# Tile 16's g transposed on TensorE instead of by DMA in a fused attention, feed-forward and soft mixture-of-experts kernel

## The chip, the cores and the metric

The kernel runs on one core of a Trainium2 chip. The time is the device time of one execution in microseconds, as the median of three runs; all times below without a unit are microseconds. Five engines work side by side, each on its own queue of instructions in program order: TensorE (PE, with its weight loads shown apart as PEld), VectorE (DVE), ScalarE (ACT), GpSimd (POOL) and SyncE (SP), which here only issues transfers.

## The reference

Three stages follow each other. Windowed causal attention over 4 batches, 8 heads, 576 positions and 64 columns a head gives x with 2304 tokens and 512 columns. A feed-forward layer of width 2048 follows, and then a soft mixture of 8 experts with 4 slots each.

```python
# attention: each query sees the 64 positions up to and including its own
attn = softmax(where(mask, q @ k.T / sqrt(D), -1e9))
x = (attn @ v)                                # 2304 x 512
# feed-forward
h = x @ w_in                                  # 2304 x 2048
g = h * tanh(log1p(exp(h)))                   # Mish
x = g @ w_out                                 # 2304 x 512
# soft mixture of experts
logits = x @ phi                              # 2304 x 32
d = softmax over tokens(logits);  slot_input = d.T @ x
slot_out[e] = relu(slot_input[e] @ w1[e]) @ w2[e]
out = softmax over slots(logits) @ slot_out
```

## The kernel before

The 2304 tokens are 18 tiles of 128, t = 0 to 17. The kernel never forms x after the feed-forward layer. It multiplies w_out by phi beforehand (wphi), so that the logits come straight from g, and it accumulates d.T @ g in A (32 slots by 2048 columns of g, kept as 128x512), to be multiplied by w_out only at the end.

For each tile TensorE makes four projections h of 128x512 (L587, twelve matmuls each, in f16 with a high and a low part). ScalarE applies Mish (L593) into u. GpSimd writes the high f16 part of g (L607), VectorE the low part (L612), both into `gg`: for each half of the 2048 columns a tile of 128 x 2 x 1024. In tile 17 this goes in pieces of 512 columns, in the others of 1024. The logits (L690, L692) need g with its columns on the partitions, `gT`, so `gg` has to be transposed. There are two ways. For tiles below `PET`, SP issues one DMA transpose for each half (`t_tr`, L618). For the others TensorE transposes 128x128 blocks into a PSUM bank (`p_tr`, L625, tiles `pghT` and `pglT`), and VectorE or ScalarE copies the bank into `gT` (`p_trev`, L630). Which of the two copies, goes by the piece's number and `VGA`.

```python
if t < P["PET"]:
    done[t, h] = [f"tr{t}_{h}"]
    op(f"tr{t}_{h}", "SP", 3.1, t0 + 12 + 2 * h, lambda t=t, h=h: t_tr(t, h), ...)
    continue
for i in mine:                       # pieces of this half
    for y, w_ in enumerate(("gh", "gl")):
        ev = "ACT" if (y == 0) == (i in P["VGA"]) else "DVE"
        op("p" + nm, "PE", 0.56 * n / 1024, t0 + 20, lambda a_=a_: p_tr(*a_), ...)
        op("v" + nm, ev, ..., lambda a_=a_, ev=ev: p_trev(*a_, ev), ...)
```

Behind the logits a softmax over tokens runs block by block. Tiles 0 to 13 make seven blocks of two, tiles 14 to 17 one block each, so that block 9 is tile 16 and block 10 is tile 17. A block goes: logits `lg` (L690, L692) to `lgt` (L696, L697, and a copy at L702), transposed into `lt` (L711, in block 10 L714), a running maximum `mrun` (L721, L724), exp (L731), the factor between the old and the new maximum (L739), transposed back as `et` (L744), split into two f16 parts (L749, L753), multiplied with g into the bank `A` (L766), and added to the accumulator (L779).

After block 10 the accumulator is transposed (At, L846) and multiplied by w_out (si, L858). Then come the experts, whose weights are 64 loads of 512 KB (`w`, L831) on SP: eh (L892, loads 0 to 31) and eo (L924, loads 32 to 63), and the output tiles fo (L977) with their stores (L989).

The order on every engine is set when the program is built. A planner (`Plan.emit`) plays the work through with estimated costs and priorities, takes the ready operation of the lowest priority number, and writes the instructions in that order. Big buffers are slots of a common pool of 49 (`s`), PSUM has 8 banks (`b`). A load can be issued only into a slot that is free in the plan, and the instruction then waits for the last reader of that slot. The slots of w_out are read last by si. Where the planner finds TensorE without ready work in certain stretches, one of them from the last projection to the first eh matmul, it writes a filler: a matmul of 128x256 into a bank of its own that nobody reads (`fill`, L194, named `pad`). Once written, a filler is an instruction like any other.

Of the kernel before, what the change touches and what calls it, by code (L numbers as in the profile page):

```python
# [24 lines left out]
PRM = dict(  # L25
    FOP=70.175, SUMA=1, XA=3, WHA=8, KEEP=7, MOSTA=0, WQ=478.64, WQ_SP=0.317, A0=-1.816, A1=6.022, AK=11,
    A2=17.918, LEAD=24.658, W0=-29.34, W_SP=5.541, W_DEC=12.468, AT=-40.0, WS=26.932, WS_SP=-0.001, T2=47.76,
    TT=15.744, WOT=72.383, WOT_SP=5.03, WO=3.842, WO_SP=1.043, NU=9, NGC=14, MOST=5, NSC=3, FAST=18, PET=17,
    SINGLE=14, MOSTL=8, LATE=31, RB=10, W2C=((0, 128), (128, 256), (384, 128)), QUART=17, VGA=[1, 3], TP=8.139,
    BL=34.953, NRM=18, VP=(-11.89, -6.08, 4.77, 5.5), CB=-54.142, KL=-1.956, NX=4, TM=(8.06, 15.01, 37.19, 38.77),  # L30
    TM_M=(-2.41, -13.01, 29.97, 14.64),
# [3 lines left out]
class Plan:  # L35
# [20 lines left out]
    def op(self, name, eng, cost, prio, fn, deps=(), get=(), rel=(), table=None, spare=False):  # L56
        assert name not in self.index, name
        self.index[name] = len(self.ops)
        need = list(Counter(p.rstrip("!^") for _, p in get).items())
        self.ops.append((name, eng, cost, prio, fn, list(deps), list(get), list(rel), table, spare, need))  # L60
        for _, p in get:
            if p[-1] in "!^":
                self.left[p] += 1
        for k in rel:
            self.refs[k] += 1
# [94 lines left out]
def body(tc, a):  # L160
# [7 lines left out]
    with ctx:  # L168
# [342 lines left out]

        TT, T2 = P["TT"], P["T2"]
        wot, wp = {}, {}
# [119 lines left out]
        for t in range(NT):  # L633
            t0 = T2 + TT * t
            last = [f"x{t // 2}"]
# [48 lines left out]
        def b_logit(b, j, h):  # L684
            n = len(BLOCKS[b])
            if j == 0 and h == 0:
                lg[b] = bank(f"lg{b}", [128, n, 64])
            t = BLOCKS[b][j]
            for k in range(8):
                PE.matmul(lg[b][:, j], lhsT=gT[t, h][:, 0, k], rhs=wphi[:, 8 * h + k], start=(h == 0 and k == 0), stop=False)  # L690
            for k in range(8):
                PE.matmul(lg[b][:, j, 0:32], lhsT=gT[t, h][:, 1, k], rhs=wphi[:, 8 * h + k, 0:32], start=False, stop=(h == 1 and k == 7))  # L692
# [88 lines left out]
        for b in range(NBLK):  # L781
            n = len(BLOCKS[b])
            e = T2 + TT * BLOCKS[b][-1] + 6 - (P["BL"] if BLOCKS[b][-1] > 15 else 0)
            late = e + 30
            prev = lambda n: [f"{n}{b - 1}"] if b else []
            two = lambda n: [f"{n}{b - 2}"] if b > 1 else []
            for j, t in enumerate(BLOCKS[b]):
                for h in range(2):
                    before = [f"lg{b}_{j}_0"] if h else [f"lg{b}_0_1"] if j else []
                    op(f"lg{b}_{j}_{h}", "PE", 0.43, e - TT * (n - 1 - j) - 2 * (1 - h), lambda b=b, j=j, h=h: b_logit(b, j, h), ["wpl"] + done[t, h] + before,  # L790
                       get=[] if before else [(f"lg{b}", "b")], rel=[f"gT{t}_{h}", f"GT{t}_{h}"])
# [14 lines left out]
            if b:  # L806
# [5 lines left out]

        TE = T2 + TT * NT
        wo, w = {}, {}
        W2C = P["W2C"]
        W2 = w2_parts(W2C)
        decode_ops("wo", a["w_out"], 16, lambda j: (j, 0), wo, lambda j: T2 + TT * (P["WO"] + P["WO_SP"] * j),
                   lambda j: T2 + TT * (P["WO"] + P["WO_SP"] * j) + 4, ["wpl"], "s", "POOL")
# [321 lines left out]
def w2_parts(cols):  # L1140

    return [(c, i, kf, 256 // d) for c, (f, d) in enumerate(cols) for i in range(2) for kf in range(0, 8, 256 // d)]
# [51 lines left out]
```

## Time and profile before

| | us |
|---|---|
| median of 3 runs | 397.94 |
| lowest and highest | 397.88, 398.8 |
| the profiled execution | 398.63 |
| its span, first to last instruction | 396.8 |

The busy times of the engines over that span are 383.6 for TensorE, 268.6 for VectorE, 275.8 for ScalarE and 97.2 for GpSimd. The mean granted clock of TensorE is 0.986 of full speed. A share of busy time is a mean over stages; what counts for a change is the stretch that it touches. Matmuls are pipelined and their ends are modelled, so the distance from one start to the next tells more than the duration of one row. In the chain of waits every step is released by the one before it, or follows it on the same engine.

### The profile page before, as it was taken

The numbers are of one execution on the slowest core, as the hardware profiler recorded it, in microseconds if no ns is written. First come the engines' busy times: TensorE is split into PE (matmuls) and PEld (weight loads), VectorE is DVE, ScalarE is ACT, GpSimd is POOL, SyncE is SP. The second block draws the span as 40 slices with busy tenths as digits, with TensorE's granted clock in tenths as the row PEclk, the third lists the DMA queues.
The fourth block names the chain that finished last, engine by engine and source line by source line (L and its number), as shares of the span: only waits on it lengthen the run. The fifth ranks groups of instructions, "written<-read, shape, count | busy, mean of one in ns | idle before, by whom it ended". The sixth has DMA issues, their size and how long they took to land.

```text
span 396.8 us, 10326 instructions
## 1 busy us (share of the span) xinstructions
PE 383.6 (97%) x4245; PEld 227.2 (57%) x4245; DVE 268.6 (68%) x579; ACT 275.8 (69%) x461; POOL 97.2 (24%) x82
## 2 busy tenths in 40 slices
PE   8999999999999999999999999999999999998982
PEld 6887758555465565566455644444454457636552
DVE  1799888879998969669899977455343374342342
ACT  1677799799986899878898399999655653102131
POOL 0243420205762222247140412121211240100000
PEclk9999999999999999999999999999999999999986
DMA  7999997131599784368999899999998889699997
GB/s 266 403 411 405 393 378 266 59 123 40 101 233 279 276 283 161 116 157 213 219 162 217 173 275 252 292 283 261 265 220 244 244 247 367 249 412 408 405 358 232
DMA packets 100686, 102.67 MB, mean 259 GB/s; under 512 B 74016, under 2 KB 81312, under 8 KB 100640
## 3 DMA queue, kind: packets, MB, share of 16 engines
q1 hardware_dynamic: 100640, 102.02, 85.9%
q8 instruction: 33, 0.54, 0.5%
q14 instruction: 13, 0.11, 0.1%
HBM read 79.46 MB, written 4.72 MB: 212 GB/s over the span
## 4 chain that ended last, share of the span: by engine, by line
PE 89%; DMA 4%; DVE 3%; issue 2%; ACT 0%; SPq 0%; DVEq 0%
PE h L587 47%; PE pad L194 6%; PE px L398 5%; PE pt L385 4%; PE eo L924 4%; PE eh L892 3%; PE s L332 3%; PE A L766 3%; DMA v<-in_vL 3%; PE lg L690 2%; PE lg L692 2%; PE fo L977 1%; DMA q<-in_qL 1%; PE gram_v L374 1%; PE s L323 1%
## 5 line engine op out<-in xcount | busy, mean ns | idle before, releaser
L587 PE MATMUL h<-wh,xx 128*128 128x512 f16 x576 | 184.3, 379 | 0.0
L587 PEld LDWEIGHTS <-xx 128*128 128x128 f16 x864 | 80.4, 98 | 86.4 <-issue 1.8
L587 PE MATMUL h<-wl,xx 128*128 128x512 f16 x288 | 109.1, 379 | 0.0
L364 POOL TENSOR_TENSOR p<-p,st 128x512 f32<-128x512 f32 x36 | 45.7, 1289 | 121.9 <-DVE st L344 34.1
L607 POOL TENSOR_SCALAR gg<-u,sc 128x1024 f16<-128x1024 f32 (+1 forms) x38 | 47.7, 1261 | 108.8 <-ACT u L593 86.1
L593 ACT ACTIVATE u<-h,sc 128x512 f32<-128x512 f32 x72 | 48.4, 686 | 28.0 <-PE h L587 23.4
L612 DVE SCALAR_TENSOR_TENSOR gg<-u,sc,gg 128x1024 f16<-128x1024 f32 (+1 forms) x38 | 50.3, 1332 | 13.8 <-POOL gg L607 13.8
L593 ACT ACT_TABLE_LOAD x41 | 52.6, 1283 | 2.0 <-PE h L587 1.3
L350 ACT ACTIVATE p<-s,st 128x128 f32<-128x128 f32 x144 | 41.8, 377 | 2.8 <-DVE st L344 2.5
L194 PE MATMUL pad<-wphi 128*64 128x256 f16 x259 | 36.5, 290 | 0.9 <-DVE wphi L204 0.9
L194 PEld LDWEIGHTS <-wphi 128*64 128x64 f16 x259 | 27.7, 116 | 5.5 <-issue 2.1
L390 ACT COPY pts<-pt 128x512 f32<-128x512 f32 x36 | 20.9, 588 | 11.4 <-PE pt L385 8.3
L341 DVE TENSOR_REDUCE st<-s 128x4 f32<-128x512 f32 x36 | 24.6, 683 | 5.4 <-PE s L332 5.4
L274 ACT ACT_TABLE_LOAD x19 | 24.4, 1283 | 1.0 <-PEq L1187 0.7
L356 DVE TENSOR_REDUCE st<-p 128x4 f32<-128x512 f32 x34 | 22.9, 674 | 2.4 <-ACT p L350 2.4
L385 PE MATMUL pt<-cst,p 128*128 128x128 f32 x144 | 21.6, 278 | 0.0
L398 PE MATMUL px<-pts,v 128*64 128x64 f32 x576 | 21.4, 225 | 0.0
L398 PEld LDWEIGHTS px<-pts,v 128*64 128x64 f32 x576 | 18.9, 138 | 3.7 <-issue 3.1
L332 PE MATMUL s<-k,q 64*64 64x128 f32 x576 | 18.8, 269 | 0.4 <-DMA q<-in_qL 0.4
L385 PEld LDWEIGHTS pt<-cst,p 128*128 128x128 f32 x144 | 16.1, 141 | 5.3 <-issue 3.0
L332 PEld LDWEIGHTS s<-k,q 64*64 64x64 f32 x576 | 16.9, 133 | 1.9 <-issue 0.7
L924 PE MATMUL eo<-w,hT 128*32 128x128 f32 (+1 forms) x384 | 16.9, 317 | 1.0 <-issue 1.0
(175 smaller groups left out, 491.8 us busy)
## 6 DMA issues: line engine op xcount, KB each, us to landing
w<-in_wL SPq DMA_DIRECT2D x64, 512.0 KB, 6.6
v<-in_vL SPq DMA_DIRECT2D x18, 512.0 KB, 8.3
wir<-in_w_in SPq DMA_DIRECT2D x16, 512.0 KB, 9.7
wtr<-in_w_outT SPq DMA_DIRECT2D x16, 512.0 KB, 4.9
wor<-in_w_out SPq DMA_DIRECT2D x16, 512.0 KB, 5.2
k<-in_kL SPq DMA_DIRECT2D x12, 512.0 KB, 8.8
q<-in_qL SPq DMA_DIRECT2D x9, 512.0 KB, 10.2
out<-ob SPq DMA_DIRECT2D x17, 256.0 KB, 3.9
```

What stands on the lines that cost most here:

```text
L194: PE.matmul(pad, lhsT=hot, rhs=hot.unsqueeze(1).to_broadcast([128, 4, 64]), start=True, stop=True)
L332: PE.matmul(st_[t][h][64 * c:64 * c + 64, p], lhsT=qt[t // 2][r, t % 2, p, 64 * c:64 * c + 64], rhs=kt[g // 3][r, p, 64 * (g % 3):64 * (g ...
L341: DVE.tensor_reduce(stat[t][:, 0, 4 * h:4 * h + 4], st_[t][h], AX.X, ALU.max)
L350: ACT.activation(pr[t][:, h, p], st_[t][h][:, p], AF.Exp, scale=0.125, bias=stat[t][:, 0, 4 * h + p:4 * h + p + 1], accum_out=(stat[t][:, ...
L364: (POOL if t < P["NRM"] else DVE).tensor_tensor(pr[t][:, h], pr[t][:, h], r, ALU.mult)
L385: PE.transpose(q[:, p], pr[t][:, h, p], ident)
L398: PE.matmul(x[64 * h:64 * h + 64, p, f], lhsT=vt[t][:, c, 64 * (2 * p + h):64 * (2 * p + h) + 64], rhs=ptS[t][:, h, p, f], start=True, sto ...
L587: PE.matmul(ph[t, m], lhsT=xh[t][:, l, kk], rhs=r[m][:, kk], start=(kk == 0 and i == 0), stop=(kk == 3 and i == 2))
L593: ACT.activation(ub[t, h][:, m % 2], ph[t, m], AF.Mish, scale=col(INVH + 4 * PART[t] + m))
L607: POOL.tensor_scalar(o, u, col(CP + PART[t]), 1.0, ALU.mult, ALU.mult)
L612: DVE.scalar_tensor_tensor(gg[t, h][:, 1, c:c + n], flat(ub[t, h], c, n), col(CP + PART[t]), gg[t, h][:, 0, c:c + n], ALU.mult, ALU.subtract,)
L924: PE.matmul(tl["o", c][32 * j:32 * j + 32], lhsT=tl[f"hT{i}"][:, 128 * (kf + k) + 32 * j:128 * (kf + k) + 32 * j + 32], rhs=v[:, j, k], st ...
```

## The change

One number changes: `PET` from 17 to 16. Tile 16's two halves are then transposed on TensorE as tile 17's are. Tile 16 has pieces of 1024 columns, so that there are four groups of 8 transposes and four evictions of 128x1024, two on VectorE and two on ScalarE. All priorities are the same as before.

```diff
-    WOT_SP=5.03, ..., MOST=5, NSC=3, FAST=18, PET=17,
+    WOT_SP=5.03, ..., MOST=5, NSC=3, FAST=18, PET=16,
```

The planner then writes another order from tile 17's second projection on. Up to there the order is the same on every engine, and from At on it is the same again.

On SP, among the weight loads, before and after (`gT_0`, `gT_1` are the two halves of tile 16):

```order
L831 DMA w_4372<-in_wL 128x1024
L618 DMA_TRANSPOSE gT_0_4392<-gg_0_4360 128x16x128
L831 DMA w_4421<-in_wL 128x1024
L831 DMA w_4458<-in_wL 128x1024
L831 DMA w_4470<-in_wL 128x1024
L618 DMA_TRANSPOSE gT_1_4483<-gg_1_4426 128x16x128
L831 DMA w_4511<-in_wL 128x1024
```

```order
L831 DMA w_4372<-in_wL 128x1024
L831 DMA w_4419<-in_wL 128x1024
L831 DMA w_4445<-in_wL 128x1024
L831 DMA w_4460<-in_wL 128x1024
L831 DMA w_4485<-in_wL 128x1024
```

The two transposes are gone, and the loads follow each other.

On ScalarE, from tile 17's first Mish on, before and after (u_0, u_1 belong to tile 17; gT_1_4496 and gT_0_4483 belong to tile 16, e_4599 and e_4565 to block 9):

```order
L593 ACTIVATE u_0_4460<-h_0_4398,sc 128x512
L593 ACTIVATE u_0_4460<-h_1_4414,sc 128x512
L593 ACTIVATE u_1_4501<-h_2_4472,sc 128x512
L593 ACTIVATE u_1_4501<-h_3_4493,sc 128x512
L630 COPY gT_0_4529<-pghT_1_4522 128x512
L630 COPY gT_0_4529<-pglT_0_4531 128x512
L630 COPY gT_1_4567<-pglT_2_4571 128x512
L630 COPY gT_1_4567<-pghT_3_4606 128x512
L731 ACT_TABLE_LOAD
L731 ACTIVATE e_4599,bst_4618<-lt_4603,mrun_76 128x128
```

```order
L593 ACTIVATE u_0_4447<-h_0_4396,sc 128x512
L593 ACTIVATE u_0_4447<-h_1_4412,sc 128x512
L630 COPY gT_1_4496<-pghT_1_4472 128x1024
L630 COPY gT_0_4483<-pglT_0_4462 128x1024
L593 ACTIVATE u_1_4536<-h_2_4500,sc 128x512
L731 ACT_TABLE_LOAD
L731 ACTIVATE e_4565,bst_4576<-lt_4568,mrun_76 128x128
L593 ACT_TABLE_LOAD
L593 ACTIVATE u_1_4536<-h_3_4554,sc 128x512
L739 ACT_TABLE_LOAD
L739 ACTIVATE bst_4576<-mrun_75,mrun_76 128x1
L630 COPY gT_0_4594<-pghT_1_4589 128x512
```

The new evictions stand ahead of the third Mish, and block 9's exp stands between the third and the fourth.

On TensorE, around block 9's lt, before and after:

```order
L194 LDWEIGHTS wphi
L194 MATMUL pad_4579<-wphi 64x256
L711 MATMUL lt_4603<-cst,e_4599 128x128
L625 LDWEIGHTS gg_1_4503
L625 MATMUL pghT_3_4606<-idh,gg_1_4503 128x128
```

```order
L587 LDWEIGHTS xx_3576
L587 MATMUL h_3_4554<-wh_1441,xx_3576 128x512
L711 MATMUL lt_4568<-cst,e_4565 128x128
L587 LDWEIGHTS xx_3576
L587 MATMUL h_3_4554<-wh_1441,xx_3576 128x512
```

It stood among fillers behind the projections, and stands between the two halves of the last projection. The 32 new transposes stand between tile 17's second and third projection. Between the last projection and At there are 61 rows of L194 before and 81 after, and between At and si there are 7 in both.

## Rows read from the trace of the kernel before

**Rows 1.** The page: TensorE's busy time, and the chain's shares by engine.

```profile
PE 383.6 (97%) x4245; PEld 227.2 (57%) x4245; DVE 268.6 (68%) x579; ACT 275.8 (69%) x461; POOL 97.2 (24%) x82
...
PE 89%; DMA 4%; DVE 3%; issue 2%; ACT 0%; SPq 0%; DVEq 0%
```

**Rows 2.** Busy time by stage; columns as in the first line.

```profile
core 0: us, PE busy (x) PEld busy (x) DVE busy (x) ACT busy (x) POOL busy (x), PEclk, DMA share, GB/s
314.00:324.60 10.60, 10.60 (x72) 4.71 (x71) 5.50 (x8) 6.80 (x8) 4.22 (x6) 1.00 0.85 236
324.60:338.30 13.70, 13.70 (x177) 10.32 (x175) 6.90 (x25) 5.38 (x12) 1.57 (x2) 1.00 0.96 354
```

**Rows 3.** The chain, 317 to 340: start, length, what.

```profile
318.30 6.48 PE h L587 x30
324.78 0.45 PE pghT L625 x8
...
327.65 0.26 PE lt L711
...
328.13 0.77 PE pad L194 x6
...
333.50 0.76 PE A L766 x12
334.26 0.17 PE et L744
334.43 1.97 PE pad L194 x17
...
337.17 1.21 PE pad L194 x10
338.38 0.59 PE At L846 x4
```

**Rows 4.** Timeline of ScalarE, 317 to 335: start, length, instruction, idle before.

```profile
318.81 1.52 ACT L593 ACTIVATE u<-h,sc 128x512 f32<-128x512 f32 x2
322.23 0.69 ACT L593 ACTIVATE u<-h,sc 128x512 f32<-128x512 f32 x1 [1.90 <-PE h L587]
...
328.77 1.28 ACT L731 ACT_TABLE_LOAD   x1
330.07 0.37 ACT L731 ACTIVATE e<-lt,mrun 128x128 f32<-128x128 f32 x1
330.33 0.19 ACT L731 ACTIVATION_READ_ACCUMULATOR e<-lt,mrun 128x1 f32 x1
```

**Rows 5.** Timeline at 359 to 361: evictions of 128x1024 f16 on VectorE and ScalarE.

```profile
359.95 0.69 DVE L1044 COPY cT<-ct 128x1024 f16<-128x1024 f16 x1
...
360.84 1.01 ACT L1044 COPY cT<-ct 128x1024 f16<-128x1024 f16 x1
```

**Rows 6.** Timeline: g of tile 17's last piece on GpSimd and VectorE.

```profile
325.60 0.69 POOL L607 TENSOR_SCALAR gg<-u,sc 128x512 f16<-128x512 f32 x1
...
327.05 0.75 DVE L612 SCALAR_TENSOR_TENSOR gg<-u,sc,gg 128x512 f16<-128x512 f32 x1
```

**Rows 7.** Timeline of SP's queue: tile 16's transposes, and loads behind si.

```profile
311.06 2.02 SPq L618 DMA_TRANSPOSE gT<-gg  x1
...
319.93 1.75 SPq L618 DMA_TRANSPOSE gT<-gg  x1
...
342.17 1.75 SPq L831 DMA_DIRECT2D w<-in_wL  x4
```

**Rows 8.** Waits of SP's queue, 330 to 348: total, times, longest.

```profile
SPq L831 <- PE si L858: 5.4, 3, 4.7
```

**Rows 9.** The line L831, 371 to 372: the last weight load.

```profile
L831 SPq DMA_DIRECT2D w<-in_wL x1: 327/327/327, 371.4 to 371.4; - x1
...
DMA to landing us min/median/max: 10.1/10.1/10.1
```

**Rows 10.** The chain, 317 to 397: a gap, and the last eo matmuls.

```profile
364.20 1.00 issue
...
384.50 1.49 PE eo L924 x48
```

More of the change, by code (lines that the diff above doesn't have):

```diff
@@ L27 @@
     A2=17.918, LEAD=24.658, W0=-29.34, W_SP=5.541, W_DEC=12.468, AT=-40.0, WS=26.932, WS_SP=-0.001, T2=47.76,
-    TT=15.744, WOT=72.383, WOT_SP=5.03, WO=3.842, WO_SP=1.043, NU=9, NGC=14, MOST=5, NSC=3, FAST=18, PET=17,
+    TT=15.744, WOT=72.383, WOT_SP=5.03, WO=3.842, WO_SP=1.043, NU=9, NGC=14, MOST=5, NSC=3, FAST=18, PET=16,
     SINGLE=14, MOSTL=8, LATE=31, RB=10, W2C=((0, 128), (128, 256), (384, 128)), QUART=17, VGA=[1, 3], TP=8.139,
```

## The prediction

> **What bounds the kernel now.** I read the page first. TensorE is busy for 97% of the span, and the chain that ended last runs on TensorE for 89% of it, against 4% on DMA [rows 1]. An average hides stages, so next I read busy time in the two stretches that the change touches: the last projections of tile 17 (314.0 to 324.6) and what follows them up to the transposition of the accumulator, At (324.6 to 338.3). In both, TensorE is busy for the whole stretch, at a granted clock of 1.00, which is the 2.4 GHz level [rows 2]. Whatever is added to TensorE's queue there is therefore paid for, unless something else in that queue becomes shorter.
>
> The second stretch needs a closer look, because much of its busy time is not work. The chain in order of time shows 30 projections in 6.48, then groups of L194 between the small steps of the softmax blocks: 6, 17 and 10 of them, for example [rows 3]. These are fillers: matmuls into a bank that nobody reads, written into the program by the planner for as long as it believes that TensorE waits. They stand in a fixed number. If the result they bridge comes early, TensorE still has to run them. So the length of this stretch is the sum of its queue as long as no real wait outlasts the fillers, and the number of fillers counts as work.
>
> Last I read what comes behind At. The weight loads of the tail (L831) wait for the si matmuls, 5.4 in all and 4.7 at the longest [rows 8]; four of them go out from 342.17 on [rows 7]. The last one leaves at 371.4 and lands 10.1 later, at 381.5 [rows 9]. TensorE reaches its last group of eo, which needs that load, at 384.50 [rows 10]: 3.0 after it is there. So the end hangs on when TensorE gets through At and si; the stream of loads is let go by the same si and follows.
>
> **The change, part by part.**
>
> *The transposes added.* Tile 16 has two halves of 2 x 1024 columns of f16, which make 32 transposes of 128x128. TensorE runs 8 of them in 0.45 in tile 17 [rows 3], so 32 take 4 x 0.45 = 1.80. They stand behind the first projections of tile 17, where TensorE has no idle time [rows 2], so all 1.80 is on the path. Those projections are not shortened by anything.
>
> *The logits and the transposed scores of block 9 (tile 16).* One half of the logits and the one lt matmul move from the stretch with fillers to before the end of the projections. They are the same instructions. Between projections a row has no filler group around it; the lt with its surroundings took 0.26 among fillers [rows 3] and cannot take less than nothing. I take no gain, and keep 0.3 of gain in the range (two group boundaries of about 0.1 each, and some of the 0.26).
>
> *The fillers.* Counting L194 from the last projection to At, the order has 61 before and 81 after; the 7 behind At stay. A group of 17 takes 1.97 and one of 10 takes 1.21 [rows 3], so a filler takes (1.97 - 1.21) / 7 = 0.109. Twenty more take 2.17. By the group of 6 in 0.77 [rows 3] a filler would be 0.128, and twenty 2.57, which I keep as the upper end. I take 0.109, since the added ones stand in groups of 4 to 16, and the number of groups hardly changes.
>
> *ScalarE.* It gets two evictions of 128x1024, each 1.01 by the nearest row, the eviction of the same shape at L1044 [rows 5]. They stand between the second and the third Mish of tile 17. In the trace there is a pause there: the pair of Mish that starts at 318.81 is over at 320.33, and the third starts at 322.23 [rows 4], when its projections are done. These now end 1.80 later for the transposes and 0.45 earlier for the half of block 9's logits that no longer stands ahead of them, so that Mish starts at about 323.6. The 2.02 of eviction, from about 320.5 on, ends at 322.6: hidden. Then the order puts block 9's exp between the third and the fourth Mish, which costs two more table loads of 1.28 [rows 4]: one to Exp, one back, with a third one to Exp after the fourth Mish in the place of the one that stood behind the evictions before.
>
> *Whether that makes TensorE wait.* The projections end at 324.78 + 1.80 + 0.45 (half the logits) + 0.11 (lt) - about 0.1 = 327.0. Block 9's lt is out at 325.7; its maximum takes VectorE about 0.8, its exp 0.37 and the accumulator read 0.2 [rows 4], so ScalarE is free at about 327.0. Table load 1.28 and Mish 0.69 [rows 4]: 329.0. GpSimd 0.69 and VectorE 0.75 [rows 6]: 330.6. TensorE needs this result for the last transposes of tile 17. In its queue it has by then, from 327.0 on: 24 transposes (1.35), 28 fillers in four groups (about 3.5), the et (0.17), block 9's A (0.76) and 4 transposes (0.3), which comes to 333.1. The result is there 2.5 earlier: hidden under fillers. If the cover failed, TensorE would wait for the difference, one for one.
>
> *VectorE.* Two evictions of 128x1024 at 0.69 [rows 5]. The first stands ahead of tile 17's first g rows, which nobody awaits until 327: hidden.
>
> *The two DMA transposes removed.* SP's queue loses 2.02 and 1.75 [rows 7], and the loads behind them go out earlier. They are loads for slots that are free already; the load that matters, the first behind si, waits for si and not for the queue [rows 8]. Nothing gained at the end.
>
> *Behind At.* The rows of every engine stand in the same order as before, and 28 loads are left when si releases them, in both. The tail moves as a whole, TensorE and the stream of loads alike, and the 3.0 between them stay.
>
> Sum: 1.80 + 2.17 = 3.97 more on TensorE ahead of At, and as much at the end. By the bounds: 1.80 + 2.17 - 0.3 = 3.7 to 1.80 + 2.57 = 4.4. The profiled execution took 398.63 with a span of 396.8 and stands 0.69 above the median, 397.94; I add the sum to the median: 401.9. What a measurement of this kernel can tell from no change is about 0.3%, or 1.2.
>
> **The rivals.**
>
> *Covered.* The added transposes run where fillers ran, and At stays at 338.38: 397.9. For it: a third of the chain from 317 to 340 is L194, which is time that could be given up. Against it: the order has more fillers, not fewer. It decides at 61 - 1.80 / 0.109 = 44 fillers ahead of At; there are 81. Chance 0.04.
>
> *Faster: one round less at the end.* Place: the stretch from the last projection to At. There block 9 and block 10 go one behind the other; with tile 16 done early, block 10 alone is left. In the order of before, 10 fillers bridge the wait ahead of block 9's A and 17 the wait from there to block 10's. Were tile 16's transposition so early that these two waits closed, the planner would write 27 fillers fewer, and by 1.21 and 1.97 for such groups [rows 3] TensorE would save 3.18 and pay 1.80: 1.4 less, 396.6. The point from which it is faster is the one above, fewer than 44 fillers ahead of At, and this rival would have 34. It also needs the fourth Mish to come at once, where the order puts it behind a table load and an exp of block 9. Chance 0.04. The Trainium skill, page "VectorE: DVE Perf Modes", section "Rules for kernel authors", speaks for this one: it sends a 128x128 transpose to TensorE wherever PSUM will do. That rule looks at one transpose, and rows 2 and 3 show a TensorE without idle time here, where each one is 0.056 of the path, so I do not follow it.
>
> *Slower still: ScalarE sets the pace.* The fourth Mish behind two table loads comes later than I worked out, by a wait in ScalarE's queue. The 2.5 of cover takes most of it. With one eviction (1.01) and two table loads (2.57) [rows 4, 5] in the way the cover falls short by 1.1: 403.0. Chance 0.13.
>
> **How the numbers follow.** The forecast, 401.9, has the rest, 0.79. Faster by over 0.3% is 0.04, within it 0.04, slower 0.92. The range takes in the sum's bounds (401.6 to 402.3), the spread of the runs before (397.88 to 398.8, so 0.9 upward), a gap like the unexplained one of 1.00 in the tail [rows 10], downward as well, and the third rival: 400.4 to 403.4.
>
> **What would show it.** Right: tile 17's last projection ends 2.2 to 2.4 later; L194 has 20 more rows, all ahead of At, and TensorE still has no idle time up to At; At starts at about 342.3; si, the loads behind it and the output follow 4 later; ScalarE has two more table loads and TensorE does not wait for them. Wrong: At later than 343 with idle time on TensorE ahead of the last transposes of tile 17 (the third rival), or an At that moved by 4 with an end that did not, which would mean that the end hung on the stream of loads in a way that I have not seen.

## The result

The changed kernel takes 403.83 (403.51 to 404.25, four executions) against 397.91 for the kernel before. The ratio is 1.0147, with a 95% interval of 1.0127 to 1.0167: 5.9 slower, where 4.0 slower was forecast with a range up to 403.4. The direction and the two terms of the sum hold; a third term of 1.5 is missing from it.

The profiled execution took 404.25, with a span of 401.4. It started 0.38 later than the one before, well ahead of the change: the group of L607 that starts at 92.90 in the kernel before starts at 93.28. Places below are compared with such an offset taken off, by that same group; for the experiments it lies between -0.29 and +1.01.

The chain of the changed kernel in order of time (start, length, what) answers to [rows 3]:

```profile
319.56 0.45 PE pghT L625 x8
...
324.83 0.23 DVE lgt L696
...
325.09 2.18 DVE lgt L697
327.29 0.24 DVE e L702
...
327.58 0.33 PE lt L711
327.91 1.29 PE h L587 x6
...
334.34 0.33 PE pghT L625 x4
...
344.51 0.59 PE At L846 x4
```

Three steps on VectorE stand in the chain between the logits of block 9 and the second half of tile 17's last projection, where TensorE alone had carried it before. At starts at 344.51, and was at 338.38 [rows 3]: with the offset taken off, 5.75 later. The busy time by stage shows the same hole (columns as in [rows 2]):

```profile
319.40:329.20 9.80, 8.32 (x93) 5.22 (x92) 7.52 (x12) 4.22 (x6) 3.97 (x5) 1.00 0.61 209
329.20:344.50 15.30, 15.30 (x181) 11.59 (x178) 6.17 (x20) 7.32 (x14) 0.69 (x1) 1.00 0.66 241
```

Of the 9.80 from the first new transpose to the end of the last projection, TensorE was busy for 8.32; in [rows 2] the stretch up to the last projection had no idle time. From there to At it is full again, at the same granted clock. The 1.48 is one wait, at block 9's lt, in the timelines of TensorE, VectorE, GpSimd and ScalarE (start, length, instruction, and in brackets the idle time before it and what ended it):

```profile
327.58 0.33 PE L711 MATMUL lt<-cst,e 128*128 128x128 f32 x1 [1.48 <-DVE e L702]
```

```profile
325.09 2.17 DVE L697 TENSOR_SCALAR lgt<-lgt,sc 128x32 f32<-128x32 f32 x1
```

```profile
324.75 0.69 POOL L607 TENSOR_SCALAR gg<-u,sc 128x512 f16<-128x512 f32 x1 [3.28 <-ACT u L593]
325.39 1.84 POOL L880 MEMSET sT<- 128x1024 f32 x2
```

```profile
328.66 1.28 ACT L731 ACT_TABLE_LOAD   x1 [3.99 <-DVE mrun L724]
...
331.72 0.69 ACT L593 ACTIVATE u<-h,sc 128x512 f32<-128x512 f32 x1
```

L697 multiplies 128x32 numbers by a factor. Its median from 200 to 345 is 0.25 in both kernels; here it took 2.17. It started while GpSimd ran L607 and ended at 327.26, 0.03 after GpSimd's second memset of sT, which ran from 325.39 to 327.23. The rows suggest that GpSimd held it. The first, the fifth and the sixth experiment test that.

### The profile page after: what moved, and what is told of

Its sections match the earlier page's. It is cut to its first block, busy times and chain, and to the rows that moved or that the text cites. A ratio compares the mean times of both kernels' runs of the same rounds, so it can differ in the third digit from the quotient of the medians.

```text
span 401.4 us, 10429 instructions
## 1 busy us (share of the span) xinstructions
PE 385.8 (96%) x4297; PEld 230.2 (57%) x4297; DVE 271.4 (68%) x581; ACT 280.0 (70%) x465; POOL 97.1 (24%) x82
## 4 chain that ended last, share of the span: by engine, by line
PE 89%; DVE 4%; DMA 3%; issue 1%; SPq 1%; ACT 0%; DVEq 0%
PE h L587 46%; PE pad L194 6%; PE px L398 4%; PE pt L385 4%; PE eo L924 4%; PE eh L892 3%; PE s L332 3%; PE A L766 3%; DMA v<-in_vL 3%; PE lg L690 2%; PE lg L692 2%; PE gram_v L374 1%; PE s L323 1%; PE fo L977 1%; DVE gg L612 1%
## 5 line engine op out<-in xcount | busy, mean ns | idle before, releaser
L607 POOL TENSOR_SCALAR gg<-u,sc 128x1024 f16<-128x1024 f32 (+1 forms) x38 | 47.7, 1261 | 115.3 <-ACT u L593 92.7
L612 DVE SCALAR_TENSOR_TENSOR gg<-u,sc,gg 128x1024 f16<-128x1024 f32 (+1 forms) x38 | 50.3, 1330 | 13.9 <-POOL gg L607 13.9
L194 PE MATMUL pad<-wphi 128*64 128x256 f16 x279 | 38.9, 288 | 0.9 <-DVE wphi L204 0.9
L194 PEld LDWEIGHTS <-wphi 128*64 128x64 f16 x279 | 29.5, 115 | 6.0 <-issue 2.6
L274 ACT ACTIVATE wiy<-wir 128x512 f32<-128x512 f32 x16 | 10.7, 690 | 8.9 <-DMA wir<-in_w_in 8.9
```

The lines of the kernel that those rows point to most:

```text
L194: PE.matmul(pad, lhsT=hot, rhs=hot.unsqueeze(1).to_broadcast([128, 4, 64]), start=True, stop=True)
L274: ACT.activation(y[j // 2][:, j % 2], raw[j][:, :, 1].bitcast(F32), AF.Prelu, scale=2.0 ** -112, alpha=2.0 ** 32)
L607: POOL.tensor_scalar(o, u, col(CP + PART[t]), 1.0, ALU.mult, ALU.mult)
L612: DVE.scalar_tensor_tensor(gg[t, h][:, 1, c:c + n], flat(ub[t, h], c, n), col(CP + PART[t]), gg[t, h][:, 0, c:c + n], ALU.mult, ALU.subtract,)
```

## The experiments

**One: the memsets elsewhere.** The planner puts GpSimd's memsets of sT behind tile 17's third piece of g, though nothing reads sT until long after. The edit lets them wait, in the plan, for block 10's accumulation; the order of the other engines does not change. In the trace they run at 332.09 and 334.94: ahead of that accumulation after all, but clear of block 9's steps on VectorE.

```diff
-op(f"sT{i}", "POOL", 0.9, f, ..., [f"mm{NT - 1}_3b"], ...)
+op(f"sT{i}", "POOL", 0.9, f, ..., [f"A{NBLK - 1}"], ...)
```

> The changed kernel (403.8) with one edit: GpSimd's two memsets of sT (L880) stand behind the accumulation of block 10 and no longer behind tile 17's third piece of g. Every other instruction keeps its place. Theory: VectorE's scaling of block 9's logits (L697) took 2.17 there and not 0.24 because it ran beside GpSimd's work, and TensorE stood still for 1.48 at block 9's transposition; without it L697 is back at about 0.24 to 0.7, TensorE has no idle time there, At comes 1.5 earlier and the time is 402.3. Rival, something else holds L697 (its input, another engine): L697 stays near 2, time 403.8. Second rival, the end doesn't hang on At: the wait goes and the time stays at 403.8.

Measured: 402.02 (401.05 to 403.56), 1.8 under the changed kernel, ratio to the kernel before 1.0102 (1.0082 to 1.0123). The line L697, and the chain (start, length, what):

```profile
L697 DVE TENSOR_SCALAR lgt<-lgt,sc x2: 242/317/392, 324.9 to 336.3; 128x32 f32<-128x32 f32 x2
```

```profile
324.56 1.30 PE h L587 x6
325.86 0.11 PE lt L711
...
342.57 0.59 PE At L846 x4
```

L697 took at most 0.39 (in block 9, where it ended 0.04 after GpSimd's L607), the lt follows its projection without a gap, and At comes 1.53 earlier with the offsets taken off. The wait is paid at the end, and the memsets are its cause.

**Two: 61 fillers.**

```diff
+count[k] += 1
+if k == 2 and count[k] % 4 == 0 and count[k] <= 80:
+    return 0.11                # the planner counts it, the program has none
 PE.matmul(pad, lhsT=hot, rhs=..., start=True, stop=True)
```

> The changed kernel with 20 fillers fewer between the last projection and At (every fourth of the first 80 isn't written), 61 as in the kernel before; all else in the same order. Theory: a filler is 0.109 on the path, At comes 2.2 earlier, the time is 401.6. Rival, ScalarE's chain (table loads and Mish) sets the pace there: TensorE waits instead, and the time stays within 0.5 of 403.8.

Measured: 402.04 (401.85 to 402.34), ratio 1.0099 (1.0086 to 1.0113). At comes 2.1 earlier than in the changed kernel; 2.17 was the term in the sum. ScalarE's chain did not take their place. The memsets stay where they were here, and the wait is there again: L697 (L701 in that kernel) took 2.17 and TensorE stood still for 1.48 at the lt.

**Three: the 32 transposes alone.** The kernel before, with the transposes ahead of the third projection of tile 17, into its bank. Nobody reads their result.

```diff
+if (t, m, half) == (17, 2, 0):
+    o = ph[t, m].bitcast(F16)
+    for h, y in ((0, 0), (0, 1), (1, 0), (1, 1)):
+        for k in range(8):
+            PE.transpose(o[:, 128*k:128*k+128], gg[16, h][:, y, 128*k:128*k+128], idh)
```

> The kernel before (397.9) with nothing but the 32 transposes of tile 16's g added on TensorE, at the place where the changed kernel has them, into the bank of the third projection, which then writes over them; no evictions, the DMA transposes stay, and the fillers stay at 61. Theory: 1.80 on the path, time 399.7. Rival, fillers cover them: the order has no fewer fillers, but if TensorE waited behind the projections for other engines, part is hidden and the time is under 399.

Measured: 400.62 (399.99 to 401.55), ratio 1.0060 (1.0046 to 1.0074), 2.4 by the ratio (1.8 to 2.9). At comes 1.95 later than in the kernel before, and the 32 stand in the chain as one group of 1.79. No filler gave way.

**Four: 81 fillers in the kernel before.**

```diff
+count[k] += 1
 PE.matmul(pad, ...)
+if k == 2 and count[k] % 3 == 0 and count[k] <= 60:
+    PE.matmul(pad, ...)
```

> The kernel before with 20 fillers more between the last projection and At (one more at every third of the first 60), 81 as in the changed kernel; all else in the same order. Theory: 2.2 on the path, time 400.1. Rival, the end hangs on the stream of weight loads and not on At: under 399.

Measured: 400.01 (399.7 to 400.19), ratio 1.0047 (1.0035 to 1.0059), 1.9 by the ratio. At comes 2.35 later. Instructions that compute nothing cost about what they last, also at the end.

These four give the account at At: 1.95 for the transposes, 2.35 for the fillers, 1.53 for the wait, together 5.83, where the changed kernel measured 5.75. With the 2.1 of run two for the fillers the sum is 5.6.

**Five: the memsets doubled.**

```diff
 POOL.memset(tl[key], 0.0)
+if key[0] == "s":
+    POOL.memset(tl[key], 0.0)
```

> The changed kernel (403.8) with each of GpSimd's two memsets of sT written twice, four in a row; all else in the same order. Theory: VectorE's L697 can't run beside GpSimd's work and waits until GpSimd's queue pauses, so it takes 2.17 + 1.84 = 4.0, TensorE stands still for 3.3 ahead of block 9's transposition, time 405.6. Rival, L697 is held by the L607 that runs when it starts, or by one memset, and slips in between two GpSimd instructions: unchanged 2.2, time 403.8. (As the last piece of tile 17's g stands behind the memsets on GpSimd but is needed much later, it is no reason for a change.)

Measured: 404.09 (403.17 to 405.33), not to be told from the changed kernel; 405.6 was expected. Timelines of VectorE and of GpSimd:

```profile
325.89 1.28 DVE L697 TENSOR_SCALAR lgt<-lgt,sc 128x32 f32<-128x32 f32 x1
327.20 1.02 DVE L702 COPY e<-lgt 128x128 f32<-128x128 f32 x1
```

```profile
326.18 0.95 POOL L880 MEMSET sT<- 128x1024 f32 x1
327.19 0.95 POOL L882 MEMSET sT<- 128x1024 f32 x1
```

My theory was too coarse. L697 slipped in when the first memset ended, at 327.13. The copy behind it started at the same moment as the second memset and was held until that one ended, at 328.14. TensorE waited 1.39 at the lt, about as long as before. So here the hold lasted until GpSimd ended an instruction, and not until its queue paused. In the changed kernel, and in run two, L697 missed the border between its two memsets; why it did there and not here, I don't know.

**Six: L697 in another form.**

```diff
-DVE.tensor_scalar(lgt[:, t:t+n], lgt[:, t:t+n], col(...), None, ALU.mult)
+DVE.tensor_tensor(lgt[:, t:t+n], lgt[:, t:t+n],
+                  col(...).unsqueeze(2).to_broadcast([128, n, 32]), ALU.mult)
```

> The changed kernel with L697 in another form, for all blocks: a tensor-tensor multiplication with the factor's column spread over the row, the same numbers, in the place of a multiplication by a per-partition scalar; memsets and all else stay where they are. Theory with the port: the form of the instruction decides; two inputs beside a memset that reads nothing run at once, L697 takes 0.3, the wait goes, time 402.2. Rival: any VectorE instruction beside the memsets is held, L697 stays at about 2.2 and the time at 403.8.

Measured: 403.9 (402.37 to 405.97), no gain. Timelines of VectorE and of GpSimd:

```profile
324.60 0.40 DVE L697 TENSOR_TENSOR lgt<-lgt,sc 128x32 f32<-128x32 f32 x1
325.03 1.79 DVE L702 COPY e<-lgt 128x128 f32<-128x128 f32 x1
```

```profile
324.90 1.84 POOL L880 MEMSET sT<- 128x1024 f32 x2
```

Half of each theory holds. In the new form L697 was not held by the memsets: it ended at 325.00, 0.1 into them. (It may have waited for the end of GpSimd's L607, 0.05 before its own.) But the next instruction, a copy of f32 from SBUF to SBUF, was held in its stead until 326.82, when the memsets ended at 326.74, and TensorE waited 1.26. Beside the memsets the form decided who was held, and two instructions in a row had such a form. Beside L607, which reads its input from SBUF, it did not: in an earlier block of the same run the new form was held as well, until 0.07 after two of GpSimd's L607 (220.50 to 222.88), and so was the old one in the kernel before (its row stands further down):

```profile
221.96 0.99 DVE L697 TENSOR_TENSOR lgt<-lgt,sc 128x64 f32<-128x64 f32 x1
```

The Trainium skill, page "SBUF — State Buffer", section "Who interferes with whom", says that VectorE in a two-port mode, which copies and tensor-scalar forms can enter and tensor-tensor forms cannot, shares a port pair with GpSimd, and that whoever comes second is blocked for the whole instruction. Beside the memsets the rows agree: 2.17, 1.02 and 1.79 for the two forms that it names as able to, 0.40 for the one that is not. No row shows the ports themselves; and coming second doesn't explain the changed kernel, where L697 stands 0.30 ahead of the first memset in the rows, rough as they are for GpSimd, and was held through both.

**Seven: both edits of one and two.**

> The changed kernel with both edits of the first two runs: memsets of sT behind block 10's accumulation, and 61 fillers. Theory: the parts add up, 403.8 - 1.8 - 1.8 = 400.2, and what is left over the kernel before is the 32 transposes. Rival: with both gone TensorE waits for ScalarE's table loads and Mish, and it stays above 401.

Measured: 400.87 (399.55 to 401.83), ratio 1.0062 (1.0041 to 1.0083). At comes 1.92 later than in the kernel before, which is what the transposes alone gave (1.95). Run three kept the two DMA transposes and this one has none, so taking them off SP's queue gained nothing that can be seen.

**Eight: the kernel before without fillers.** One of the 68 up to si is left.

```diff
+count[k] += 1
+if k == 2 and count[k] > 1:
+    return 0.11
 PE.matmul(pad, ...)
```

> The kernel before (397.9) without the fillers between the last projection and si (one is left, for the bank). Shows what the fillers cover there. If they only bridge real waits, At stays at 338.3 and the clock decides: with waits of 1 to 2 the granted clock may fall to half, and si and eh, 17 long at full clock, would be up to twice as long, time up to 410. If the fillers overshoot, At comes earlier by 2 to 5 and, at full clock, the time is 393 to 396. My forecast's premise (the fillers are longer than the waits) wants the second for At.

Measured: 395.63 (394.91 to 396.49), ratio 0.9930 (0.9903 to 0.9956): faster than both kernels. Busy time by stage, and the chain (the edit shifts the line numbers by 4, here and in the runs below):

```profile
324.60:332.60 8.00, 6.70 (x109) 4.54 (x106) 5.31 (x19) 5.39 (x12) 2.32 (x3) 1.00 0.96 379
332.60:339.40 6.80, 4.68 (x34) 2.13 (x38) 2.69 (x11) 0.37 (x1) 0.00 (x0) 0.50 0.99 393
```

```profile
333.35 1.50 PE A L770 x12
...
335.67 1.13 PE At L850 x4
...
337.30 4.05 PE si L862 x48
```

At came 3.2 earlier: the fillers outlast the waits by that much, as the forecast had assumed. And TensorE's granted clock was at 0.50 of full speed, the 1.2 GHz level, from 332.6 to 339.4. Before it fell, TensorE had waited for 0.68 and for 0.28 and had just begun a wait of 0.81. The second block's A took 1.50 and At 1.13 there, against 0.76 and 0.59 [rows 3]. So the fillers outlast the waits, and without them the clock fell.

**Nine: the changed kernel without fillers**, memsets late as in the first run.

> The changed kernel with the memsets of sT late, as in the first run, and without the fillers up to si (one is left). Against the kernel before without fillers (395.6, At at 335.1 on the clock of the kernel before). The prediction's second rival was that tile 16 on TensorE takes one round out of the end once fillers don't cover it. By the first run's rows the fourth Mish starts at about 328.2, the last g is there at 330.4, and from there transposition, eviction, logits, reduction, exp and two accumulations lead to At at about 336: 1 later than without the change, time 396.6. Rival, one round less: At at 333 to 334, time under 395.

Measured: 402.61 (399.73 to 403.12), ratio 1.0100 (1.0071 to 1.0130). The chain:

```profile
332.37 1.47 ACT gT L634 x3
...
337.49 1.50 PE A L770 x8
...
339.82 1.13 PE At L850 x4
```

At comes at 339.8, which is 4.7 later than in the kernel before without fillers; I had expected 1. The stretch from 328 to 346 ran at a granted clock of 0.62, so some of the 4.7 is the clock. TensorE's own pieces of this chain from 332.37 to At are 3.16 in all; at full clock they would be about half of that (an estimate, by A with 1.50 against 0.76), which leaves At about 3 later than in run eight. The chain goes through ScalarE's copies of tile 17's transposes, which in the new order stand behind block 9's exp, the fourth Mish and the table loads between them. The other 4.3 of the chain are ScalarE's, VectorE's and issue, so that even with nothing for TensorE's pieces At would be at 336.6, where the rival needs 333 to 334. That kills the second rival: with fillers out of the way, tile 16 on TensorE does not take a round out of the end, it makes the end longer.

**Ten and eleven: fewer fillers in the kernel before.** Every third of them, or 29 left where run eight showed waits.

```diff
+if k == 2 and count[k] % 3 != 1:                  # ten
+if k == 2 and not any(lo <= count[k] < hi for lo, hi in      # eleven
+        ((1, 2), (17, 21), (24, 29), (35, 43), (52, 58), (62, 67))):
+    return 0.11
```

> The kernel before with every third of the fillers up to si (23 of 68). If 61 fillers overshoot by what the run without fillers showed (At 3.2 earlier), a third of them is still under the waits: At 3 earlier as there, and, as TensorE pauses less, the clock may stay up through At and si (there it fell to half and si took 4.05 in place of 2.88): time 393 to 395.6. If a third already outlasts the waits: above 395.6.

> The kernel before with 29 of the 68 fillers, left where the run without fillers showed TensorE waiting: none ahead of the last transposes and logits of tile 17, 4 ahead of block 10's lt, 5 and 8 around the two blocks' accumulations, 6 ahead of At, 5 ahead of si. Theory: nothing of them outlasts a wait, the clock stays up, At at 335 and si at full clock, time 393 to 395, better than both kernels. Rival, the clock falls all the same: as without fillers, 395.6.

Measured: 395.31 (394.7 to 396.33), ratio 0.9940 (0.9923 to 0.9957), for the third, and 394.21 (393.64 to 396.14), ratio 0.9915 (0.9892 to 0.9938), for the 29. The stretch up to At in run ten and in run eleven, and the chain of run eleven:

```profile
324.60:335.00 10.40, 9.61 (x139) 6.34 (x136) 6.76 (x25) 5.35 (x12) 1.32 (x2) 1.00 1.01 397
324.60:335.00 10.40, 10.02 (x143) 6.95 (x141) 6.97 (x26) 5.39 (x12) 1.85 (x3) 1.00 1.02 401
```

```profile
334.91 0.66 PE At L850 x4
...
336.23 3.10 PE si L862 x48
```

In run eleven the clock stays at 1.00, up to 342, At comes as early as without fillers, and si takes 3.10 in place of 4.05. Its median is the lowest here, 3.4 under the kernel before by the ratio; its interval overlaps with those of runs eight and ten. In run ten, with 23 fillers spread evenly, the clock stays at 1.00 as well, and At comes 3.6 earlier than in the kernel before, sooner than in run eleven. So the places of the 29 are not shown to matter; in the profiled executions what lies between ten and eleven comes behind At, and its cause is open.

## Why the prediction was right or wrong

*What bounds the kernel: right.* TensorE's queue up to At set the time, and fillers counted as work. Runs two, four, eight and eleven show it from both sides.

*The transposes, 1.80: right.* In the changed kernel they go in four groups of 0.45, and alone they moved At by 1.95. That the DMA transposes taken away gain nothing was right too: run seven against run three.

*The fillers, 2.17: right*, with 2.1 and 2.35 in the two runs that change their number.

*The logits and the lt, no gain: wrong, and this is the step that failed.* I priced the lt by its own length and gave it a place between two projections, where TensorE has no slack, without asking what it waits for there. Before, it stood among fillers, and nothing held VectorE's three steps ahead of it: they took 0.75 from 326.39 on, with GpSimd's memsets over since 325.48, and were done about 0.5 before TensorE came to the lt. VectorE and GpSimd in the kernel before, first in an early block and then in block 9:

```profile
222.07 0.96 DVE L697 TENSOR_SCALAR lgt<-lgt,sc 128x64 f32<-128x64 f32 x1
...
326.63 0.24 DVE L697 TENSOR_SCALAR lgt<-lgt,sc 128x32 f32<-128x32 f32 x1
```

```profile
220.61 2.38 POOL L607 TENSOR_SCALAR gg<-u,sc 128x1024 f16<-128x1024 f32 x2
...
323.64 1.84 POOL L880 MEMSET sT<- 128x1024 f32 x2
```

In its new place the projections cover 1.3 from the logits on. The three steps took 2.7, and the rest was a wait of 1.48, after which the lt itself took 0.33 where run one has 0.11. Tile 17's last projection ended 4.0 later, where I had given 2.2 to 2.4 as the sign of being right. The paragraph on ScalarE then set out from "block 9's lt is out at 325.7"; it started at 327.2 and was out at 327.5 with the offset taken off. In the paragraph on VectorE I counted the two evictions and left out the steps of block 9, which moved too. And no part of the working went through GpSimd's queue, where the memsets stand beside them. L697 and GpSimd's L880 both have rows in the trace of before, and I used neither. The sign was there: the L697 at 222.07 took 0.96, and ended 0.04 after two of GpSimd's L607.

*The cover on ScalarE's side: right.* The fourth Mish came at 331.7, 3.0 later than worked out with the offset taken off. Of that, 1.8 is the late lt. Most of the rest, 1.28, is that the table load ahead of block 9's exp waits for the maximum as the exp does (3.99 idle, put down to mrun), where I had let it run ahead; the load at 312.14 in the kernel before ends such a wait too. But TensorE had no idle time from the last projection to At: the fillers covered even this. Of the 2.5 of cover about 1.2 was left: GpSimd's part of the last g was there at 333.19, and its transposes began at 334.34. In run nine, without fillers, TensorE did wait for that part, for 1.10.

*The rivals.* "Covered" and "faster" are out: run three shows the transposes in full, and run nine that the round at the end does not go away. "Slower still" came near in size, 403.0, by luck, since it had the wrong place. It was to be ScalarE's table loads ahead of the last transposes; it was VectorE, ahead of block 9's lt, and not under fillers.

*The tail: right in the sum, not in its parts.* I let the tail move as a whole. At moved by 5.75 and the end of the span by 4.2, both with the offset taken off. TensorE reaches the last eo at 387.84, in the chain that ends last, against 384.50 [rows 10]: 3.0 later only, as a gap of 1.00 in eo is not there any more, and the granted clock from the first output tile on was higher. A stretch of 8 from about 40 behind At, before and after:

```profile
379.00:387.00 8.00, 7.22 (x115) 4.34 (x113) 3.44 (x6) 3.44 (x5) 0.00 (x0) 0.81 1.05 344
```

```profile
384.00:392.00 8.00, 6.16 (x118) 4.10 (x115) 3.94 (x10) 3.69 (x6) 0.00 (x0) 1.00 1.09 364
```

In both the DMA engines are busy throughout. The loads are let go by si and the stores stand behind them in the same queue, which, as I read it, keeps the end close to At, whatever TensorE gains in between; no run tests that. Over six profiled executions, from the kernel before to run four, the end of the span lies 57.0 to 59.1 behind At; in the other seven it is 57.2 to 61.3, the most in run nine, whose si took 4.99. What else moves it is open. So is the time outside the span, 1.83 in the profiled execution before and 2.85 in this one (1.77 to 2.49 in the other three), which makes up for what the span lacks in the 5.6 between the two.

## What to carry to other kernels

An instruction that moves from a stretch with slack to one without has to be priced with everything it waits for in the new place: each engine on the way to it, and what the neighbours of that engine do at that time. Fillers in a fixed order are work: take their number from the order, and look whether they outlast the waits that they bridge; 68 in place of 29 cost this kernel 3.4, and the 29, or 23 spread evenly, still kept the clock up. Work that nobody awaits, like zeroing a buffer, should stand where no short link of a chain runs on VectorE. Where a short instruction takes several times its usual length somewhere in the trace of before, and ends together with one of another engine, it is worth finding out why before forecasting.

## What the runs showed of the hardware

GpSimd's memsets of 128x1024 f32, 0.95 each, held VectorE's f32 tensor-scalar and its f32 copy from SBUF to SBUF: up to 2.17 for an instruction of 0.25, over two memsets, and up to 1.79 for one of 0.23. The held rows ended 0.03 to 0.08 after a row of GpSimd. A tensor-tensor form ended 0.1 into such a memset, after 0.40, but beside GpSimd's L607 it took up to 0.99. Not held by the memsets in the kernel before (323.64 to 325.48) were L612, a scalar-tensor-tensor form (0.75 at 323.74), and L630, a copy out of PSUM (0.42 at 325.05): both as long there as elsewhere. TensorE's granted clock fell to 0.50 in run eight after waits of 0.68 and 0.28 and as one of 0.81 began. In run ten, with waits of 0.35, 0.30 and 0.18, and in run eleven it stayed at 1.00.
